# Attention with a token and channel mixer: q and k transposed by VectorE, scores as 32-row tiles, mixer input transposed by DMA

## The chip, the cores and the metric

The kernel runs on one core of one Trainium2 chip. The metric is the time of one execution on the device in microseconds (us); where a kernel ran several times, the median is quoted. Engine names in the profiles: PE is TensorE (PEld its weight loads), DVE is VectorE, ACT is ScalarE, POOL is GpSimd, and SP is the engine that issues most DMA transfers. In this kernel PE writes its results into PSUM, from where DVE or ACT copies them to tiles in SBUF. The clock of PE is given as the share of full speed that it was granted. Batches are counted from 0 here; the recorded expectations of the experiments count them from 1. One run of the kernel before took 840.59 us; it is left out of every ratio, but the medians 341.17 and 340.29 us on record still count it (without it they are 340.5 and 340.0). Runs marked slow (over 1.5% above the fastest of the same kernel) are left out of every ratio.

## The reference, cut to what matters

Eight batches of eight heads of causal attention with a decay that accumulates along the sequence (S = 576, D = 64), followed per batch by a mixer over tokens and one over channels.

```python
# shortened
scores = scale * np.matmul(q, k.transpose(0, 1, 3, 2))          # [8, 8, 576, 576]
cum = np.cumsum(np.maximum(s, 0.0), axis=-1)
bias = -(cum[:, :, :, None] - cum[:, :, None, :])
scores = np.where(causal, -1e9, scores + np.minimum(bias, 0.0))
attn = exp(scores - max); attn = attn / (sum + 1e-09)
x = np.matmul(attn, v)                                          # then heads side by side: [8, 576, 512]
# mixer
h  = np.maximum(x.T @ w_tok1, 0.0) @ w_tok2                     # w_tok1 576x256, w_tok2 256x576
u  = x + h.T
out = u + np.maximum(u @ w_ch1, 0.0) @ w_ch2                    # w_ch1 512x1536, w_ch2 1536x512
```

The kernel computes only two diagonals of 128x128 blocks of the attention (farther positions have decayed away, which a check at the end confirms; the squares of q and k serve that check).

## The kernel before

A small planner in the kernel takes every operation with its allowed engines and an estimate of its time, chooses the engine where there is a choice, and fixes the order of each engine before anything runs. The order cannot adapt when an operation takes longer than the estimate.

q and k are loaded for two heads, cast to bf16 (by GpSimd from batch 1 on), transposed by PE and copied out of PSUM by DVE or ACT:

```python
    def stage_qk(b, h):                      # two heads
        ...
            alts = {"POOL": (*c_pool(768, 0.0010), lambda cast=cast: cast(0))}
            if b == 0:
                alts["DVE"] = (*c_dve(768), lambda cast=cast: cast(1))
                alts["ACT"] = (*c_act(768), lambda cast=cast: cast(2))
    def pair(b, h):
        ...
                for r in range(R):           # R = 6
                    nc.tensor.transpose(out=o[:, r * PR : (r + 1) * PR],
                                        in_=nat.t[:, ti, r, :, :].rearrange("p e d -> p (e d)"), ...)
        ...                                  # kT and qT copied out of PSUM
                    nc.tensor.matmul(out=o[:, :, c0 : c0 + e - a], lhsT=kT.t[:, j0 : j0 + 128],
                                     rhs=qT.t[:, :, a:e], start=True, stop=True)
        ...                                  # Exp by ACT, then the causal mask by DVE:
                    nc.vector.tensor_tensor(
                        out=E.t[:, :, d0 : d0 + n], in0=E.t[:, :, d0 : d0 + n],
                        in1=keep[:, k0 : k0 + n].unsqueeze(1).to_broadcast([128, 2, n]), op=ALU.mult)
```

The score matmul uses all 128 rows of PE: the two heads lie above each other in kT, and qT holds zeros in the half of the other head. The causal mask reads two tensors in SBUF, E and keep. The input of the channel mixer (u transposed) is made by PE transposes and copies out of PSUM.

## Time and profile before

| | before |
|---|---|
| time, median | 341.17 us in the runs given (see above), 340.0 to 340.5 beside the experiments |
| span of the profiled run | 337.3 us |
| PE busy, PE idle | 315.2 us, 22.1 us |
| DVE / ACT / POOL busy | 207.7 / 221.6 / 100.1 us |
| first matmul of the channel mixer | 41.27 us |

Before the first matmul of the channel mixer PE also runs dummy matmuls, which are meant only to keep its clock up (no run here goes without them), so "PE busy" says little there. I therefore cut the time line at that matmul. In the view of the kernel before by stretches, the columns are the stretch, its length, then busy time and count of PE, PEld, DVE, ACT and POOL, the granted PE clock, the share of the DMA engines and GB/s:

```profile
41.27:110.00 68.73, 64.93 (x616) 43.33 (x620) 50.94 (x119) 50.97 (x94) 41.19 (x48) 1.00 0.91 207
110.00:230.00 120.00, 116.28 (x922) 65.53 (x935) 75.45 (x184) 84.36 (x147) 36.78 (x47) 1.00 0.51 132
230.00:337.30 107.30, 99.27 (x709) 56.51 (x716) 46.63 (x116) 59.16 (x110) 3.25 (x4) 1.00 0.26 79
```

Length minus PE busy is PE's idle time: 3.8, 3.7 and 8.0 us, together 15.6 us. PE is the bound after 41 us. The clock is full. One group of the same page: a third of the causal masks (those on one of three buffers), with count, busy time in us and mean in ns, then DVE's idle time before them:

```profile
L671 DVE TENSOR_TENSOR E_84<-E_84,keep 128x256 bf16<-128x256 bf16 (+1 forms) x55 | 18.4, 365 | 13.3 <-ACT E_84 L663 12.8
```

DVE waits for ACT's Exp before these masks. The masks are ready early enough that PE hardly waits for them: in the view of PE's waits the masks have two lines (total us, times, longest), 0.9 us together:

```profile
PE pav_115 L689 <- DVE E_84 L671: 0.6, 2, 0.3
...
PE pav_115 L689 <- DVE E_86 L671: 0.3, 1, 0.3
```

### The profile page before, as it was taken

The page shows a single profiled execution, that of the slowest core. Times are in us where ns is not written, and L with a number is a line of the kernel's source. Part 1 is how long each engine was busy: PE and PEld are TensorE (multiplying, and loading weights), DVE is VectorE, ACT ScalarE, POOL GpSimd, SP SyncE. Part 2 cuts the span into 40 slices and gives each one's busy share as a digit, 9 for nine tenths or more (in the row PEclk, how much of TensorE's full clock was granted, in tenths as well). Part 3 has the DMA queues.
Part 4 walks back from the last instruction along what each step waited for, and adds up shares of the span by engine and source line. Part 5 has one row for each costly group of instructions (what it writes and reads, how often), then busy time and mean ns, then how long its engine had stood idle before and what let it go on. Part 6 is the DMA issues. An engine that isn't in the chain of part 4 may idle for free.

```text
span 337.3 us, 6710 instructions
## 1 busy us (share of the span) xinstructions
PE 315.2 (93%) x2532; PEld 184.7 (55%) x2565; DVE 207.7 (62%) x510; ACT 221.6 (66%) x395; POOL 100.1 (30%) x137
## 2 busy tenths in 40 slices
PE   6978999988999999989999999989999999999992
PEld 2445585645765455555765445555765454446641
DVE  7698945899776746584577655584677545450021
ACT  4766975669788548785786747787799738325600
POOL 6355157768237001830147001830110000000000
PEclk9799999999999999999999999999999999999999
DMA  7999999999953349288024952253548110011031
GB/s 203 222 291 376 374 213 231 266 271 227 215 114 106 130 138 206 77 208 194 2 75 133 227 145 71 87 157 121 143 119 232 67 63 2 16 49 62 3 95 68
DMA packets 62584, 50.60 MB, mean 150 GB/s; under 512 B 39632, under 2 KB 55568, under 8 KB 62544
## 3 DMA queue, kind: packets, MB, share of 16 engines
q1 hardware_dynamic: 62544, 50.10, 56.7%
q8 instruction: 22, 0.36, 0.4%
q14 instruction: 18, 0.15, 0.2%
HBM read 40.65 MB, written 9.44 MB: 148 GB/s over the span
## 4 chain that ended last, share of the span: by engine, by line
PE 69%; DVE 18%; ACT 7%; issue 2%; DMA 1%; POOL 1%; SPq 0%; ACTq 0%
PE pmx_118 L877 9%; PE pmx_119 L877 8%; PE pmx_117 L859 8%; PE pmx_118 L859 8%; PE pmx_119 L859 8%; PE pmx_117 L877 7%; DVE ub_101 L819 3%; PE pmx_119 L791 2%; DVE E_86 L671 2%; PE psc_114 L657 2%; PE pav_115 L689 2%; PE psc_113 L657 2%; DVE E_84 L671 2%; PE pav_116 L689 2%; PE psc_112 L657 2%
## 5 line engine op out<-in xcount | busy, mean ns | idle before, releaser
L859 PEld LDWEIGHTS <-wc_70 128*128 128x128 bf16 x624 | 59.3, 98 | 30.5 <-issue 0.2
L877 PEld LDWEIGHTS <-gb_107 128*128 128x128 bf16 x240 | 22.9, 98 | 25.3
L575 POOL CAST qkn_76<-qkf_73 96x768 bf16<-96x768 f32 x22 | 19.1, 887 | 37.5 <-ACT gb_107 L866 20.1
L877 PEld LDWEIGHTS <-ga_106 128*128 128x128 bf16 x192 | 18.2, 98 | 21.2 <-issue 1.4
L575 POOL CAST qkn_77<-qkf_74 96x768 bf16<-96x768 f32 x19 | 15.7, 840 | 40.8 <-ACT ga_106 L866 19.7
L575 POOL CAST qkn_75<-qkf_72 96x768 bf16<-96x768 f32 x19 | 15.4, 828 | 39.1 <-ACT gb_107 L866 18.5
L671 DVE TENSOR_TENSOR E_84<-E_84,keep 128x256 bf16<-128x256 bf16 (+1 forms) x55 | 18.4, 365 | 13.3 <-ACT E_84 L663 12.8
L859 PE MATMUL pmx_118<-uTb_105,wc_70 128*128 128x320 bf16 x128 | 22.6, 299 | 0.1
L859 PE MATMUL pmx_117<-uTb_105,wc_70 128*128 128x320 bf16 x128 | 22.6, 299 | 0.0
L859 PE MATMUL pmx_119<-uTb_105,wc_70 128*128 128x320 bf16 x128 | 22.6, 299 | 0.0
L877 PE MATMUL pmx_119<-wc_71,gb_107 128*128 128x512 bf16 x92 | 22.3, 379 | 0.2
L548 POOL TENSOR_TENSOR vp_90<-vf_88,wT 128x512 bf16<-128x512 f32 (+1 forms) x20 | 21.0, 1069 | 2.5 <-DMA vf_88<-in_v_dram 2.2
L671 DVE TENSOR_TENSOR E_86<-E_86,keep 128x256 bf16<-128x256 bf16 (+1 forms) x50 | 17.1, 368 | 6.7 <-ACT E_86 L663 6.4
L671 DVE TENSOR_TENSOR E_85<-E_85,keep 128x256 bf16<-128x256 bf16 (+1 forms) x55 | 16.5, 329 | 6.3 <-ACT E_85 L663 6.1
L877 PE MATMUL pmx_118<-wc_71,gb_107 128*128 128x512 bf16 x80 | 19.2, 379 | 0.2
L866 ACT ACTIVATE gb_107<-pmx_119 128x320 bf16<-128x320 f32 x25 | 11.1, 444 | 11.4 <-PE pmx_119 L859 9.9
L859 PE MATMUL pmx_118<-uTa_104,wc_70 128*128 128x512 bf16 (+1 forms) x77 | 17.0, 335 | 0.2
L859 PE MATMUL pmx_119<-uTa_104,wc_70 128*128 128x512 bf16 (+1 forms) x79 | 17.1, 336 | 0.1
L548 POOL TENSOR_TENSOR vp_89<-vf_87,wT 128x512 bf16<-128x512 f32 (+1 forms) x15 | 15.3, 1040 | 5.8 <-PE pav_116 L689 4.7
L859 PE MATMUL pmx_117<-uTa_104,wc_70 128*128 128x512 bf16 (+1 forms) x78 | 16.8, 335 | 0.1
L877 PE MATMUL pmx_117<-wc_71,ga_106 128*128 128x512 bf16 x69 | 16.7, 379 | 0.2
L877 PE MATMUL pmx_118<-wc_71,ga_106 128*128 128x512 bf16 x69 | 16.5, 379 | 0.3 <-ACT uTb_105 L839 0.2
(297 smaller groups left out, 723.0 us busy)
## 6 DMA issues: line engine op xcount, KB each, us to landing
qkf_74<-in_k_dram SPq DMA_DIRECT2D x15, 288.0 KB, 3.4
qkf_74<-in_q_dram SPq DMA_DIRECT2D x15, 288.0 KB, 4.0
vf_87<-in_v_dram SPq DMA_DIRECT2D x16, 256.0 KB, 7.0
vf_88<-in_v_dram SPq DMA_DIRECT2D x16, 256.0 KB, 5.5
qkf_72<-in_k_dram SPq DMA_DIRECT2D x13, 288.0 KB, 4.0
qkf_72<-in_q_dram SPq DMA_DIRECT2D x13, 288.0 KB, 4.5
qkf_73<-in_k_dram SPq DMA_DIRECT2D x12, 288.0 KB, 4.7
qkf_73<-in_q_dram SPq DMA_DIRECT2D x12, 288.0 KB, 5.0
```

Of the source, the lines that this page charges most:

```text
L548: eng.tensor_tensor(out=vp.t[p0 : p0 + n, c, :, 0:D], in0=vf.t[p0 : p0 + n, c, :, :], in1=wT[p0 : p0 + n, cw, b * H : b * H + H].unsqueeze ...
L575: nc.gpsimd.tensor_copy(out=o, in_=a)
L657: nc.tensor.matmul(out=o[:, :, c0 : c0 + e - a], lhsT=kT.t[:, j0 : j0 + 128], rhs=qT.t[:, :, a:e], start=True, stop=True)
L671: nc.vector.tensor_tensor(out=E.t[:, :, d0 : d0 + n], in0=E.t[:, :, d0 : d0 + n], in1=keep[:, k0 : k0 + n].unsqueeze(1).to_broadcast([128, ...
L689: nc.tensor.matmul(out=o[:, ic, 0 : D + 1], lhsT=E.t[:, hh, d0 : d0 + 128], rhs=vp.t[:, jc, h + hh, 0 : D + 1], start=(jc == j_lo), stop=( ...
L791: nc.tensor.matmul(out=pm.t[:, ha * D : hb * D], lhsT=w1[:, NJ if odd and c == NJ - 1 else c, t * 128 : t * 128 + 128], rhs=x.t[:, c, ha * ...
L819: nc.vector.tensor_tensor(out=dst.t[lo:hi, di, :], in0=pm.t[lo:hi, :], in1=x.t[lo:hi, c, :], op=ALU.add)
L859: nc.tensor.matmul(out=pm.t[:, 0 : e - a], lhsT=wc1[:, m, cc * 128 : cc * 128 + 128], rhs=uT.t[:, m, a:e], start=(m == 0), stop=(m == NMC ...
L866: lambda cc=cc, pm=pm, a=a, e=e: nc.scalar.activation(out=g.t[:, cc, a:e], in_=pm.t[:, 0 : e - a], func=AF.Relu),
L877: nc.tensor.matmul(out=pm.t[:, :], lhsT=g.t[:, cc, c * 128 : c * 128 + 128], rhs=wc2[:, cc, :], start=(cc == 0), stop=(cc == NCC - 1))
```

## The change

The intent is to take work off PE. VectorE transposes q and k in 32x32 blocks, which leaves 32 of the 64 head elements on 32 partitions. Four heads therefore lie on the four row groups of PE, and each head's scores are two matmuls of 32 rows, accumulated in PSUM, that can run beside those of the other heads. The transposing, the rounding to bf16 and the reordering of the sequence are divided differently: the cast now also undoes the order of the loaded rows. From batch 2 on the mixer input is transposed by DMA.

```diff
-    R = 6
-    PR = S // R
+    UDMA = 2
+    HQ = 4
+    TP = 128 // HQ
+    R = S // TP
+    DQ = D // 32
 ...
     def stage_qk(b, h):
+        for i in range(2):
 ...
+            P.op(dve(R * D, lambda f=f, t1=t1: nc.vector.transpose(
+                out=t1.t[:, :, :, :].rearrange("p r q t -> p (r q t)"), in_=f.t[:, :])),
+                reads=[(f, 0)], writes=[(t1, 0)], holds=[T], prio=2 if b else -1)
+            for qq in range(DQ):
+                def cast(e, qq=qq, t1=t1, T=T):
+                    o = T.t[:, qq, 0:S].rearrange("p (t r) -> p t r", r=R)
+                    a = t1.t[:, :, qq, :].rearrange("p r t -> p t r")
+                    if e == 0:
+                        nc.gpsimd.tensor_copy(out=o, in_=a)
 ...
+                alts = {"POOL": (*c_pool(S, 0.0017), lambda cast=cast: cast(0))}
 ...
+                for (jc, a, z, c0) in cols:
+                    for qq in range(DQ):
+                        for e in range(HQ):
+                            p0 = e * TP
+                            nc.tensor.matmul(out=ps[e].t[:, c0 : c0 + z - a],
+                                             lhsT=kT.t[p0 : p0 + TP, qq, jc * 128 : jc * 128 + 128],
+                                             rhs=qT.t[p0 : p0 + TP, qq, a:z], start=(qq == 0), stop=(qq == DQ - 1),
+                                             tile_position=(p0, 0))
 ...
-                        in1=keep[:, k0 : k0 + n].unsqueeze(1).to_broadcast([128, 2, n]), op=ALU.mult)
+                        in1=keep[:, 0:n].unsqueeze(1).to_broadcast([128, HQ, n]), op=ALU.mult)
 ...
+            if b >= UDMA:
+                def xt(dst=dst, di=di, tc_=tc_):
+                    nc.sync.dma_start_transpose(out=uT.t[:, :, tc_ * 128 : tc_ * 128 + 128], in_=dst.t[:, di, :])
```

The diff also changes the loads (four heads at a time, fewer and larger packets), the squares (taken of the loaded fp32 values) and the number of buffers.

The read of the new cast steps 256 bytes from element to element: 18 values r, each a block of 64 fp32 apart. The write is contiguous.

## The prediction

> **What bounds the kernel now.** I first read the page's shares and slices, to see whether one engine is full.
>
> ```profile
> PE 315.2 (93%) x2532; PEld 184.7 (55%) x2565; DVE 207.7 (62%) x510; ACT 221.6 (66%) x395; POOL 100.1 (30%) x137
> ...
> PE   6978999988999999989999999989999999999992
> ...
> DMA  7999999999953349288024952253548110011031
> ```
>
> TensorE (PE) is busy 93% of the 337.3 us span, no other engine more than 66%. The DMA engines are full only in the first eleven slices (to about 93 us). So there are two stages. I checked this in the windows, whose columns are the stretch, its length, busy time and count of PE, PEld, DVE, ACT and POOL, the granted clock, the DMA share and GB/s:
>
> ```profile
> 0.00:20.00 20.00, 16.47 (x98) 7.79 (x100) 15.06 (x43) 12.42 (x21) 9.54 (x27) 0.91 1.03 224
> 20.00:40.00 20.00, 16.96 (x190) 11.00 (x191) 18.40 (x46) 13.47 (x24) 9.29 (x12) 1.00 1.03 351
> ...
> 160.00:180.00 20.00, 19.95 (x182) 13.50 (x182) 11.50 (x30) 15.09 (x31) 7.78 (x9) 1.00 0.20 60
> ```
>
> From 80 to 320 us PE is busy 234 of 240 us (sum of the twelve windows): there, each microsecond of PE work removed is a microsecond of time, as long as nothing else starts to wait. The first 41 us are different. The groups of line L964 are dummy matmuls on zeros that only keep the clock up; they sum to 19.1 us, all before 41.2 us. PE is not the limit there; the chain of waits between 5 and 32 us goes through VectorE (DVE) and ScalarE (ACT): casts, q/k evictions, Exp, mask, normalisation of batch 0. The first real mixer matmul (L859) starts at 41.27 us.
>
> What one piece of PE work really costs is not in the group means (they contain the pipeline's latency) but in the pieces of the chain of waits; the columns are start, length, engine, tile, line, count:
>
> ```profile
> 29.95 0.29 PE pav_115 L689 x9
> ...
> 32.38 0.26 PE psc_114 L619 x6
> 32.64 0.22 PE psc_112 L657
> 32.85 0.22 PE psc_113 L657
> ...
> 34.67 0.22 PE psc_114 L657
> 34.88 0.22 PE psc_112 L657 x2
> ...
> 37.82 0.22 PE pmx_119 L831 x4
> ```
>
> Six q/k transposes take 0.26 us, a 512-column score matmul 0.22, the last two (384 and 128 columns) 0.22 together, four transposes of the mixer input 0.22. The nine attention-value matmuls take 0.29, that is 32 ns for a weight load with its matmul, so weight loads can follow one another at least that fast.
>
> **What the skill says.** (1) "TensorE: Matmul & The Clock Gate", Part 3, gives 3.07x for four 32-row tiles at 512 columns, and says such matmuls overlap when each is in its own row group. No run here shows it yet. (2) "TensorEngine Tiling (Array Packing)", Key Properties: changing the tiling mode drains TensorE. The trace has no tiled matmul; its matmuls of 512 columns last 379 ns and follow each other every 216, so a drain is about 0.16 us. (3) "Vector Engine (DVE) Microarchitecture Reference", 3.8: the 32x32 transpose sustains one element per cycle and lane. The trace has none, but other one-rate operations: the 512-element products (L548) take 0.68 us, the 320-element ones (L703) 0.49, so 1.0 ns an element and 0.17 fixed. (4) "Advanced Engine Details and Errata", X-Bar Transpose (TRN2): transposing DMAs are as fast as plain ones. The trace has none.
>
> **The change, part by part.**
>
> *PE, scores.* Before, one pair of heads costs 2 x 0.26 + 4 x 0.22 = 1.40 us, four heads 2.80. After, q/k transposes leave PE altogether. Four heads are 40 matmuls of 32 rows: for each of two halves of the head's 64 elements 256+256+256+192+64 = 1024 columns on four row tiles. One tile alone would take 2 x 1024/2.4 GHz = 0.85 us; at 3.07 of the ideal 4, 1.11 us (an estimate from (1)). 40 loads at 32 ns give 1.28 as the other limit, from the trace. Two phases with a change of mode in and out are 4 drains of up to 0.16; I take half of them as exposed, 0.3. That is 1.4 to 1.6 us, say 1.5: saved 1.3 per four heads. Batch 0 lies before the matmuls that count, and three of the four pairs of batch 1 ran before 41 us beside dummies, so I count 12 of 16 groups: 12 x 1.3 = 15.6 us.
>
> *PE, mixer input.* Batches 2 to 7 have 3 x (4 + 5) = 27 tiles; each loses 0.22 us: 5.9 us, all in the full stage.
>
> *DVE and ACT.* Evictions of q/k: 36 on DVE at 0.75 and 60 on ACT at 0.64, 27 + 38 = 65 us, go. Evictions of the mixer input: 27 of 36 go (19 on ACT at 0.59, 17 on DVE at 0.41 in all), about 13.5 us. Squares: 32 x (1.48 + 0.19) = 53.5 becomes 32 x (1.48 x 1152/1536 + 0.19) = 41.6, minus 12. Masks: half as many, twice as wide; 160 at 0.33 are 52 us, and the 0.07 or so of fixed cost saved on 80 is 6 to 10. Added: 32 DVE transposes of 1152 elements at 0.17 + 1.15 = 1.32, plus 42 us. DVE and ACT together fall from 429 to about 375. Neither comes near the PE's some 290.
>
> *GpSimd.* 60 casts of 0.84 us (50 us) become some 56 strided ones of 576 elements. At the measured 1.08 ns an element they are 35 us; with the kernel's own allowance for strided reads 60. POOL goes to at most 115 of 310 us and stays off the path.
>
> *DMA.* The page has 62,584 packets, of which the 15,360 of q and k have 1536 bytes; afterwards there are 5,120 of 4608. By the kernel's own allowance two heads' k and q fall from 2.26 to 1.65 us, some 24 us of DMA time in all, of which six loads (about 3.5 us) lie ahead of the mixer's weights. Against that come 27 transposes of 128 KB.
>
> *Start.* Batch 0 loses two transposes and three evictions per pair from a chain that DVE and ACT bound, and gains four DVE transposes. Loads of 0.6 MB land near 5.5 and 7.2 us, first scores near 9.5 (before: 11.44), and four phases of four Exps (0.49 us apart in the timeline at 13 us) end near 20 to 21. I expect the normalised attention of batch 0 some 4 us earlier than 31.6, and the weights some 3.5 us earlier, so the first mixer matmul at about 37: 4 us.
>
> *New waits.* PE gets four score banks per phase and a phase fills all four, so phases follow at 2.5 us at best; with mixer work between, this is mostly hidden. A transposing DMA is issued in order on SyncE behind loads like these:
>
> ```profile
> 51.22 8.03 SPq L539 DMA_DIRECT2D vf_87<-in_v_dram  x5
> ```
>
> Five loads of v hold that queue for 8 us, while PE's order is fixed beforehand. I charge 4 us for late mixer input and score banks.
>
> Sum: 15.6 + 5.9 + 4 - 4 = 21.5 us. The median before is 341.17 (the 840.59 run is set aside), so 319.5.
>
> **The rivals.** (a) Row tiles do not overlap. Then four heads cost 4 x 0.85 + 0.3 = 3.7 us instead of 2.8: 12 x 0.9 = 11 us lost, with 5.9 + 4 - 4 gained: 346, within 2%. For it: no run here shows the overlap; against it: the skill's measured factor, and each tile has its own bank. (b) Mixer input arrives late: at 4 us of stall in each of six batches, 24 us instead of 4, leaving 339.5. For it: the 8 us above and the DMA share of 1 up to 93 us; against it: the DMA share falls to 0.2 to 0.7 after 100 us, and chan() of a batch is ranked behind two batches' attention, so other PE work stands in front. (c) Vector work becomes the bound: transposes of 1.32 us get between the masks and PE. Against it: 375 us on two engines over 320 us of span. If it does happen early (DVE is 18.40 of 20 us busy at 20 to 40 us), the start gives nothing: 323.5. (d) Everything overlaps and waits vanish too: 1.2 us per four heads, no new waits, 6 us at the start: 12 x 1.6 + 5.9 + 6 = 31, so 310.
>
> **Range and chances.** The sure part is PE work leaving a full PE. Centre 319; (d) with a little more gives 307, half of (b) with (c) gives 332. Faster by over 2% means below 334.3: it needs (a) or a full (b) to fail, 0.87. Within 2% 0.10, slower 0.03.
>
> **What would show it.** The 32-row matmuls of four heads spanning 1.4 to 1.6 us in two phases (3.7 would be rival a); PE busy time falling by 25 to 45 us with its idle time not up; the first L859-type matmul near 37 us; DVE transposes at 1.3 us; waits of the up-projection on the mixer-input DMA below 1 us each (several us would be rival b). The prediction fails if PE idle time after 80 us exceeds some 15 us, before about 6.

## The result and the profile after

The changed kernel took 323.82 us (median of five, 319.96 to 324.48), the kernel before beside it 340.29 us (340.0 without the run set aside). The ratio is 0.950, with a 95% interval of 0.944 to 0.955. Ratios here are the mean time of one kernel's fast runs over that of the other's in the same rounds, so not quite the ratio of the medians quoted. The profiled run happened to be the fastest of the five (span 318.2 us, clock 0.986); the others have spans of 320.4 to 322.6 us at a clock of 0.965 to 0.971.

The page of the changed kernel, first the busy times, then the slices of PE, its clock and DMA:

```profile
PE 288.5 (91%) x2550; PEld 162.1 (51%) x2550; DVE 220.6 (69%) x415; ACT 168.2 (53%) x319; POOL 121.7 (38%) x129
...
PE   7879999497888997998999999998899999999992
...
PEclk9999999798999999999999999999999999999998
DMA  7999999993797864024970597136960520050032
```

PE lost 26.7 us of work and ACT 53.4, while DVE and POOL gained 12.9 and 21.6. But in slices 8 to 19 (of 8 us each, so about 56 to 151 us) the row of PE has a 4, two 7s and four 8s, where the row before had three 8s and nothing below. PE's idle time in the whole span rose from 22.1 to 29.7 us. The same stretches as before, cut at the first mixer matmul, which is now at 33.57 us:

```profile
0.00:33.57 33.57, 27.94 (x284) 14.85 (x285) 30.46 (x70) 19.49 (x29) 16.11 (x29) 1.00 0.98 326
33.57:110.00 76.43, 66.05 (x726) 42.66 (x724) 66.91 (x121) 54.61 (x110) 53.89 (x51) 0.96 0.90 240
110.00:230.00 120.00, 112.65 (x970) 60.41 (x968) 88.37 (x148) 61.62 (x119) 51.59 (x49) 1.00 0.54 148
230.00:318.20 88.20, 81.81 (x575) 44.15 (x575) 34.84 (x79) 32.45 (x64) 0.08 (x1) 0.99 0.26 80
```

From the two tables the whole difference of the spans can be put together. The first mixer matmul is 7.7 us earlier. PE's busy time after it falls from 280.5 to 260.5 us, by 20.0. PE's idle time after it rises from 15.6 to 24.1 us, by 8.6 (10.4, 7.4 and 6.4 in the three stretches). -7.7 - 20.0 + 8.6 = -19.1 us, which is 337.3 to 318.2. This is bookkeeping, not yet a cause: an earlier start can be lost again in later waits.

What does PE wait for? The view of PE's waits in the changed kernel (total us, times, longest):

```profile
PE pmx L656 <- DVE E L638: 8.6, 9, 2.1
PE pmx L656 <- DVE x L670: 3.6, 2, 3.4
```

L656 is the attention-value matmul, L638 the causal mask. The masks are now the largest wait of PE; neither GpSimd nor a transposing DMA has a line in that view. And yet half as many masks, each twice as wide, should have been cheaper. The groups of the changed kernel that matter:

```profile
L582 POOL CAST kT<-qkt 128x576 bf16<-128x576 f32 x31 | 36.7, 1212 | 87.8 <-DVE qkt L574 76.0
...
L638 DVE TENSOR_TENSOR E<-E,keep 128x512 bf16<-128x512 bf16 (+1 forms) x80 | 55.0, 734 | 3.3 <-ACT E L631 3.2
```

The mask takes 734 ns in the mean. Its own view (shortest/median/longest in ns) shows that the mean is not typical:

```profile
L638 DVE TENSOR_TENSOR E<-E,keep x80: 273/426/1683, 14.2 to 266.1; 128x512 bf16<-128x512 bf16 x64, 128x256 bf16<-128x256 bf16 x16
```

Half of them take 426 ns or less, others up to four times that. The timeline around the deepest dip of PE shows when (start, length in us, engine, line, count; in brackets the idle time before it and its releaser):

```profile
54.86 2.30 POOL L582 CAST kT<-qkt 128x576 bf16<-128x576 f32 x2 [2.07 <-PE pmx L656]
56.63 3.26 DVE L638 TENSOR_TENSOR E<-E,keep 128x512 bf16<-128x512 bf16 x3
57.11 2.63 POOL L582 CAST qT<-qkt 128x576 bf16<-128x576 f32 x2
...
60.42 0.32 PE L656 MATMUL pmx<-vp,E 128*128 128x65 bf16 x3 [3.40 <-DVE x L670]
```

Three masks take 3.26 us, 1.09 each, while GpSimd casts run from 54.86 to 59.74. Behind them the normalisation (L670) is late, and PE stands still for 3.40 us. Just behind this gap the granted clock of PE was lower as well:

```profile
60.00:65.00 5.00, 4.58 (x59) 3.15 (x59) 3.93 (x13) 1.94 (x5) 5.00 (x7) 0.66 1.10 358
```

The Trainium skill, "SBUF — State Buffer", section "Who interferes with whom", names this: a VectorE instruction with two SBUF inputs contends with a GpSimd instruction that reads SBUF, because its second input comes through an interface that the two share. The mask is such an instruction and the cast such a reader; the timeline agrees, with 1.09 us against the median of 0.43.

The trace can settle this mask by mask. I sorted the 80 masks, from the start and length of each instruction in the trace, by whether a GpSimd cast or product was running when they started. The 35 beside none took 0.27 to 0.43 us. The other 45 took 1.00 us in the mean, and every one of them ended 0.15 to 0.31 us after that GpSimd instruction ended, however much of it was left. Of these 45, 31 started beside a cast of q or k, 10 beside a product for v and 4 beside other casts. So a mask that starts during such a GpSimd instruction waits for its end, and a longer one makes it wait longer. The kernel before shows the same on fewer masks: 30 of 160, with 0.71 us in the mean against 0.27.

The score phases did what was hoped. Timeline of PE in the changed kernel:

```profile
48.75 0.61 PE L622 MATMUL psc<-qT,kT 32*128 32x256 bf16 x16
49.30 2.76 PE L849 MATMUL pmx<-wc,ga 128*128 128x512 bf16 x12
51.99 0.62 PE L622 MATMUL psc<-qT,kT 32*128 32x256 bf16 x24
52.55 0.82 PE L849 MATMUL pmx<-wc,ga 128*128 128x512 bf16 x3
```

From the start of a phase to the start of the next matmul there are 0.55 and 0.56 us. Entering a phase costs some 0.1 us more: the 12 matmuls from 49.30 us, at 216 ns each, should be followed at 51.89, and the phase begins at 51.99. That is about 1.3 us for four heads, where the prediction's reading of the kernel before gave 2.80.

### The profile page after: what moved, and what is told of

Its sections match the earlier page's. It is cut to its first block, busy times and chain, and to the rows that moved or that the text cites. A ratio compares the mean times of both kernels' runs of the same rounds, so it can differ in the third digit from the quotient of the medians.

```text
span 318.2 us, 6568 instructions
## 1 busy us (share of the span) xinstructions
PE 288.5 (91%) x2550; PEld 162.1 (51%) x2550; DVE 220.6 (69%) x415; ACT 168.2 (53%) x319; POOL 121.7 (38%) x129
## 4 chain that ended last, share of the span: by engine, by line
PE 58%; DVE 27%; DMA 5%; issue 5%; SPq 1%; ACT 1%; DVEq 0%; ACTq 0%
PE pmx L831 23%; PE pmx L849 19%; DVE E L638 9%; DVE qkt L574 7%; PE pmx L758 5%; PE pmx L656 4%; DMA qkf<-in_q_dram 4%; PE psc L622 3%; PE pmx L779 2%; DVE ub L786 2%; DVE of L860 2%; DVE x L670 2%; DMA qkf<-in_k_dram 2%; DVE vp L543 1%; DVE ua L786 1%
## 5 line engine op out<-in xcount | busy, mean ns | idle before, releaser
L631 ACT ACTIVATE E<-psc 128x512 bf16<-128x512 f32 x128 | 66.1, 607 | 53.9 <-PE psc L622 53.9
L831 PEld LDWEIGHTS <-wc 128*128 128x128 bf16 x624 | 60.4, 98 | 35.9 <-issue 3.4
L831 PE MATMUL pmx<-uTb,wc 128*128 128x320 bf16 x384 | 55.0, 301 | 2.6 <-DVE gb L840 1.5
L638 DVE TENSOR_TENSOR E<-E,keep 128x512 bf16<-128x512 bf16 (+1 forms) x80 | 55.0, 734 | 3.3 <-ACT E L631 3.2
L849 PE MATMUL pmx<-wc,gb 128*128 128x512 bf16 x240 | 53.5, 379 | 0.0
L565 ACT ACTIVATE junk<-qkf 128x1152 bf16<-128x1152 f32 x32 | 37.6, 1174 | 14.1 <-DMA qkf<-in_k_dram 12.5
L849 PE MATMUL pmx<-wc,ga 128*128 128x512 bf16 x192 | 43.6, 379 | 0.0
L831 PE MATMUL pmx<-uTa,wc 128*128 128x512 bf16 (+1 forms) x240 | 43.5, 337 | 0.0
L574 DVE STREAM_TRANSPOSE qkt<-qkf 128x1152 f32<-128x1152 f32 x32 | 43.1, 1360 | 0.5 <-DMA qkf<-in_q_dram 0.2
L656 PE MATMUL pmx<-vp,E 128*128 128x65 bf16 x576 | 26.2, 196 | 16.9 <-DVE E L638 8.6
L543 POOL TENSOR_TENSOR vp<-vf,wT 128x512 bf16<-128x512 f32 (+1 forms) x35 | 37.1, 1090 | 8.7 <-PE pmx L656 8.7
L849 PEld LDWEIGHTS <-gb 128*128 128x128 bf16 x240 | 22.9, 98 | 26.7
L838 ACT ACTIVATE gb<-pmx 128x320 bf16<-128x320 f32 x58 | 24.9, 445 | 21.6 <-PE pmx L831 17.9
L656 PEld LDWEIGHTS <-E 128*128 128x128 bf16 x576 | 22.1, 99 | 24.3 <-issue 11.2
L670 DVE TENSOR_TENSOR x<-pmx,rc 128x320 bf16<-128x320 f32 x64 | 29.3, 484 | 0.8
L860 DVE TENSOR_TENSOR of<-pmx,ub 128x512 f32<-128x512 f32 x16 | 10.8, 687 | 15.0 <-PE pmx L849 12.9
## 6 DMA issues: line engine op xcount, KB each, us to landing
ga<-in_moe_w_ch_dram SPq DMA_DIRECT2D x2, 768.0 KB, 12.9
```

The lines of the kernel that those rows point to most:

```text
L543: eng.tensor_tensor(out=vp.t[0:n, c, :, 0:D], in0=vf.t[0:n, c, :, :], in1=wT[0:n, c, b * H : b * H + H].unsqueeze(2).to_broadcast([n, H, D ...
L565: P.op({"ACT": (1.1, 1.5, lambda: nc.scalar.activation(out=junk[:, :], in_=f.t[:, :], func=AF.Square, accum_out=sq[:, col : col + 1]))}, r ...
L574: P.op(dve(R * D, lambda f=f, t1=t1: nc.vector.transpose(out=t1.t[:, :, :, :].rearrange("p r q t -> p (r q t)"), in_=f.t[:, :])), reads=[( ...
L631: nc.scalar.activation(out=E.t[:, e, ph * 512 : ph * 512 + 512], in_=p.t[:, :], func=AF.Exp, scale=0.125)
L638: nc.vector.tensor_tensor(out=E.t[:, :, d0 : d0 + n], in0=E.t[:, :, d0 : d0 + n], in1=keep[:, 0:n].unsqueeze(1).to_broadcast([128, HQ, n]) ...
L656: nc.tensor.matmul(out=o[:, ic, 0 : D + 1], lhsT=E.t[:, hh, d0 : d0 + 128], rhs=vp.t[:, jc, h + hh, 0 : D + 1], start=(jc == j_lo), stop=( ...
```

## The experiments

The theory: the casts of q and k on GpSimd slow VectorE's masks beside them, and late masks leave PE idle. The main rival: something else that came with the change delays VectorE or PE, such as the 1.36 us transposes in front of the masks, late DMA transposes, or GpSimd itself being too slow for the scores. There were twelve runs, one of them the changed kernel again. The record marks every result as right, even that of casts_straight, which scrambles q and k. So this check does not notice a wrong order of q and k, and for the other runs that order rests on the code. The runs are ordered by question. Each has its own kernel-before runs of the same chip beside it (340.0 to 340.5 us in the median).

### Do the casts slow the masks?

**casts_act.** From batch 1 on ScalarE makes the casts, alone.

```diff
                 alts = {"POOL": (*c_pool(S, 0.0017), lambda cast=cast: cast(0))}
+                if b > 0:
+                    alts = {"ACT": (1.2, 1.4, lambda cast=cast: cast(2))}
```

> The changed kernel with the q/k casts of batches 2 to 8 on ScalarE in place of GpSimd. Theory (contention): the masks on VectorE take 0.73 us in the mean and 0.43 in the median because a GpSimd cast runs beside them; without casts on GpSimd their mean falls to about 0.5 (the v products still run there), VectorE busy falls by 15 us or more, and TensorE's idle time between 33 and 110 us falls from 10.4 to about 5; ratio to the kernel before near 0.935. Rival (VectorE is simply full with 32 transposes ahead of the masks in its order): the masks get shorter but TensorE's idle time stays above 9 us and the ratio stays at 0.95. Against both: ScalarE gains 56 casts of 1.2 us (67 us), so late Exps could take the gain back.

Measured: 312.61 us, ratio to the kernel before 0.919 (0.916 to 0.922). Its page, with the mask on line 640:

```profile
PE 285.8 (92%) x2520; PEld 161.6 (52%) x2549; DVE 219.1 (70%) x446; ACT 212.1 (68%) x344; POOL 54.4 (17%) x73
...
L640 DVE TENSOR_TENSOR E<-E,keep 128x512 bf16<-128x512 bf16 (+1 forms) x80 | 36.9, 510 | 6.9 <-ACT E L633 6.9
```

The mask's mean falls to 510 ns (80 take 36.9 us instead of 55.0). PE is idle 7.2 instead of 10.4 us between 33.57 and 110 us. ACT carries 44 us more and still does not become a bound. The gain is larger than forecast (0.935), but one forecast failed: DVE's busy time was to fall by 15 us or more and fell by 1.5. The masks did take 18.1 us less, but the new plan gave DVE 31 more instructions (446 against 415). It is 3 to 4% under the changed kernel and, within the noise, as fast as any run. One point against reading the start as decisive: its first mixer matmul comes at 38.94 us, 5.4 us later than in the changed kernel, and it ends 7 us earlier (profiled spans 311.2 and 318.2). The planner ordered everything anew here, though, so this run alone does not prove the mechanism.

**casts_half.** Only the casts of q go to ScalarE.

```diff
-                alts = {"POOL": (*c_pool(S, 0.0017), lambda cast=cast: cast(0))}
+                alts = {"POOL": (*c_pool(S, 0.0020), lambda cast=cast: cast(0))}
+                if b > 0 and i == 1:
+                    alts = {"ACT": (1.2, 1.4, lambda cast=cast: cast(2))}
```

> The changed kernel with the q casts (28 of 56) of batches 2 to 8 on ScalarE and the k casts left on GpSimd. Contention theory: mask mean near 0.6 us and about half of the gain of the run with all casts moved, unless ScalarE becomes late there, in which case this one is the fastest of the three: ratio 0.935 to 0.945. Rival (VectorE full): 0.95, unchanged.

Measured: 313.49 us, 0.924 (0.920 to 0.927); the mask's mean is 595 ns. Half the casts off GpSimd brings over 60% of the mask time back and most of the gain; the forecast of 0.935 to 0.945 was too cautious.

**after_again and casts_straight.** The control is the changed kernel itself. In casts_straight GpSimd reads and writes straight ahead, in the same number of elements, so that its casts become short; nothing is planned anew, every engine has the same instructions in the same order. What it computes is wrong.

```diff
-                        nc.gpsimd.tensor_copy(out=o, in_=a)
+                        nc.gpsimd.tensor_copy(
+                            out=T.t[:, qq, 0:S],
+                            in_=t1.t[:, :, :, :].rearrange("p r q t -> p (r q t)")[:, qq * S : qq * S + S])
```

> The changed kernel itself once more, as the control on this chip: a ratio of 0.950 to the kernel before, clock near 0.97, TensorE idle some 10 us between 33 and 110 us. Both theories expect the same.

> Wrong result on purpose: the GpSimd casts of q and k read and write straight through instead of in the strided order, with the same plan, the same order on every engine and the same number of instructions. A straight cast of 576 elements should take 0.6 to 0.7 us instead of 1.25. Theory (GpSimd casts beside the masks make them slow, not the order or the load of VectorE): with half the GpSimd cast time the mask mean falls from 0.73 to about 0.6 us and the ratio to 0.935 or 0.94 though nothing was re-planned. Rival (the run with the casts on ScalarE won because its plan put the instructions in another order): mask mean and ratio stay at 0.72 and 0.95. The scores are of scrambled q and k, which changes no instruction's size.

Measured: after_again 321.91 us, 0.948 (0.941 to 0.955), as in the first runs. casts_straight 312.57 us, 0.921 (0.914 to 0.929), better than the forecast of 0.935 or 0.94. The groups of casts_straight (the mask is on line 640 here):

```profile
L582 POOL CAST kT<-qkt 128x576 bf16<-128x576 f32 x31 | 20.2, 682 | 97.6 <-DVE qkt L574 88.0
...
L640 DVE TENSOR_TENSOR E<-E,keep 128x512 bf16<-128x512 bf16 (+1 forms) x80 | 43.3, 589 | 3.5 <-ACT E L633 3.3
```

Only GpSimd's casts were shortened, and DVE's masks became 11.7 us shorter. DVE's whole busy time fell by 11.9 us, so nothing else on DVE moved. Sorted as above, 35 masks instead of 45 start beside a GpSimd instruction, and they take 0.84 us instead of 1.00; those beside none take 0.40 us. The transposes, the DMAs and the order are the same, so the rivals that rest on them cannot explain it. The stretches of casts_straight:

```profile
33.57:110.00 76.43, 69.83 (x746) 44.40 (x743) 65.75 (x124) 55.30 (x111) 43.56 (x55) 0.96 0.90 245
110.00:230.00 120.00, 116.21 (x1032) 64.24 (x1030) 86.09 (x166) 66.66 (x128) 35.10 (x46) 1.00 0.57 163
```

PE is idle 6.6 and 3.8 us here, instead of 10.4 and 7.4: 7.4 of the 8.1 us by which the profiled spans differ (318.2 and 310.1). Both profiled runs have nearly the same mean clock (0.986 and 0.987). PE's waits for masks are halved, 4.3 us. What remains of the theory's rivals is that GpSimd itself was late; but the changed kernel's list of waits has no line of PE waiting for a cast on GpSimd, and DVE stood idle only 3.3 us before all its masks (3.5 in casts_straight), so it was not waiting for late scores either. This run settles it: the length of the casts beside the masks cost the changed kernel about 8 to 9 us (8.1 between the profiled runs, 9.3 between the medians). What the remaining overlap costs, with short casts and with the products for v, no run isolates.

**before_casts_act.** Is moving casts off GpSimd simply a good thing? The same on the kernel before, whose casts of 768 elements read runs of 64 neighbours.

```diff
             alts = {"POOL": (*c_pool(768, 0.0010), lambda cast=cast: cast(0))}
+            if b > 0:
+                alts = {"ACT": (0.85, 1.05, lambda cast=cast: cast(2))}
```

> The kernel before with its q/k casts of batches 2 to 8 on ScalarE too. Theory: the change itself made the contention matter, since there the masks take 0.33 us in the mean against 0.29 in the median and TensorE is full, so this gives nothing: ratio 0.99 to 1.01, or a little slower as ScalarE is the fuller engine there. Rival (moving casts off GpSimd is a gain of its own, unrelated to the change): ratio 0.97 to 0.98.

Measured: 338.29 us, 0.994 (0.988 to 1.000), as forecast; the mask's mean is 307 ns (354 in the kernel before, from its three groups). There PE waited only 0.9 us for masks, so shorter masks bring almost nothing. The slowing of masks was there already; that it costs time is new in the changed kernel.

**casts_order and casts_half_order.** The other way to write the same cast: read 32 fp32 side by side, write every 18th bf16. The idea was to make the cast shorter; casts_half_order does it with q's casts on ScalarE.

```diff
-                    o = T.t[:, qq, 0:S].rearrange("p (t r) -> p t r", r=R)
-                    a = t1.t[:, :, qq, :].rearrange("p r t -> p t r")
+                    o = T.t[:, qq, 0:S].rearrange("p (t r) -> p r t", r=R)
+                    a = t1.t[:, :, qq, :]
```

> The changed kernel, right result and same plan, with the two loops of each q/k cast exchanged: it now reads 32 neighbouring float32 and writes every 18th bf16, in place of reading every 64th float32 and writing 18 neighbours. If the far reads are what makes a GpSimd cast 1.25 us against 0.73 for a straight one, it takes 0.7 to 0.8 us now and the kernel behaves as the straight one did: mask mean near 0.6 us, ratio 0.92. If far writes cost as much as far reads, the casts stay at 1.2 us and the ratio at 0.948.

> Both at once: loops of the casts exchanged, and the q casts of batches 2 to 8 on ScalarE. If each removes GpSimd time beside the masks, the mask mean falls to 0.52 to 0.55 us, TensorE's idle time between 33 and 110 us falls below 7 us, and the ratio is 0.912 to 0.920, the best so far; if what is left is VectorE's own work, it stays at 0.92 as in the straight run.

Measured: 364.41 us, 1.070 (1.065 to 1.076; one slow run left out) and 352.44 us, 1.035 (1.029 to 1.040). Both are slower than the kernel before. The groups of casts_order:

```profile
L582 POOL CAST kT<-qkt 128x576 bf16<-128x576 f32 x31 | 80.8, 2805 | 73.0 <-DVE qkt L574 59.9
...
L638 DVE TENSOR_TENSOR E<-E,keep 128x512 bf16<-128x512 bf16 (+1 forms) x80 | 69.7, 918 | 3.2 <-ACT E L631 3.2
```

The hope fell: writing every 36 bytes makes the cast 2.3 times as long, and not on GpSimd alone, as ScalarE takes 2.77 us and VectorE 2.70 us for it. As a test of the theory the run is of use, because the dose went the other way. With GpSimd casts of 0.73, 1.25 and 2.84 us (mean of k and q) the mask's mean is 589, 734 and 918 ns. The time is not as clean here: in casts_order PE also waits 19.0 us for GpSimd's casts themselves, so its 1.070 is two effects. Nor does a mask wait for the end of such a cast here: masks that start beside one end up to 2.6 us before it, so the rule found above holds for the casts with far reads and not for these. Of casts_half_order's forecasts none came true; its mask mean is 767 ns.

### What is each part of the change worth?

**x_all_pe.** The changed kernel with PE transposes of the mixer input in all batches.

```diff
-    UDMA = 2
+    UDMA = 8
```

> The changed kernel with every transpose of the mixer input back on TensorE (none by DMA). Theory: the DMA transposes land in 2.5 us and nobody waits for them, so taking them away gives back their TensorE work, 27 x 0.22 = 5.9 us, a ratio near 0.967 against 0.950. Rival: TensorE idles some 10 us after 110 us anyway because VectorE is late, so the 5.9 us are hidden and the ratio stays within 0.945 to 0.955; or the extra evictions on VectorE and ScalarE make it cost more than 6 us.

Measured: 328.34 us, 0.965 (0.962 to 0.968). By the ratios (0.948 and 0.950 for the changed kernel) the DMA transposes are worth about 5 to 6 us on top of the scores part, as forecast.

**before_x_dma.** The kernel before, with the DMA transposes alone.

```diff
+            if b >= 2:
+                def xt(dst=dst, di=di, tc_=tc_):
+                    nc.sync.dma_start_transpose(out=uT.t[:, :, tc_ * 128 : tc_ * 128 + 128], in_=dst.t[:, di, :])
+                P.op({"SP": (1.3, 0, xt)}, reads=rk, writes=[(uT, c)], holds=[uT], prio=0, dma=0.7)
+                continue
```

> The kernel before with only the third part of the change: mixer input of batches 3 to 8 transposed by DMA. Theory: TensorE is full there from 80 us on, so the 27 x 0.22 us that leave it show one to one, 5.9 us or ratio 0.983, if nobody waits for the DMA; it was worth 1.5% in the changed kernel. Rival: in this kernel the loads hold the queue in other places, and the up-projections wait for late input: ratio 0.995 or more and waits of the up-projection on the DMA of a microsecond or more each.

Measured: 327.69 us, 0.963 (0.957 to 0.968): 12.5 us, twice what was expected, and a miss. Its page:

```profile
PE 309.0 (95%) x2457; PEld 178.0 (55%) x2457; DVE 208.1 (64%) x512; ACT 207.2 (64%) x366; POOL 102.2 (31%) x137
```

PE's busy time falls by 6.2 us, which is the predicted 5.9. The profiled spans differ by 11.5 us (337.3 and 325.8), so PE's idle time falls by the other 5.3, from 22.1 to 16.8. The parts are therefore not additive: the scores part alone brings 11.7 us (340.02 to 328.34, from x_all_pe), the DMA part alone 12.5, both together 16 to 18. Most of the saved idle time lies between 110 and 230 us, where PE is idle 0.5 us instead of 3.7. Which waits go there, and why, was not followed further and stays open.

### Do the row tiles overlap?

**tiles_in_turn.** The same score matmuls, but one head's tile after the other instead of turn by turn.

```diff
-                for (jc, a, z, c0) in cols:
-                    for qq in range(DQ):
-                        for e in range(HQ):
-                            p0 = e * TP
+                for e in range(HQ):
+                    for (jc, a, z, c0) in cols:
+                        for qq in range(DQ):
+                            p0 = e * TP
```

> The changed kernel with the same 40 score matmuls per four heads, but ordered head by head, so that neighbours use the same 32 rows of the array. Theory (the row tiles overlap, and that is what keeps the scores cheap): a phase that takes 0.55 us grows to near 2 x 4 x 512 columns / 2.4 GHz = 1.7 us; 12 groups of two phases on the full stage lose up to 2 x 1.15 x 12 = 28 us, less what the idle time absorbs: ratio 1.00 to 1.04. Rival (the matmuls hardly overlap; the gain is from the transposes that left TensorE): phases stay at 0.55 to 0.7 us and the ratio stays near 0.95.

Measured: 328.75 us, 0.968 (0.965 to 0.972), between the forecasts. The phase of 16 matmuls stays nearly as it was (mostly 0.58 us instead of 0.55). The phase of 24 more than doubles; timeline of PE in tiles_in_turn:

```profile
114.19 1.32 PE L622 MATMUL psc<-qT,kT 32*128 32x256 bf16 x24
115.45 0.82 PE L849 MATMUL pmx<-wc,gb 128*128 128x512 bf16 x3
```

It takes 1.26 us instead of 0.56. Without any overlap, 16 matmuls of 256 columns would need 1.7 us: matmuls of 512 columns follow each other every 216 ns in the kernel before (this is also the 2.4 GHz of the recorded texts), so 256 need about 0.108. The phase of 24 has as many columns in all. A phase of 0.56 us is thus overlap in fact, and it survives a head-by-head order with four matmuls of 256 columns per tile, but not with six of 256, 192 and 64. A queue of limited depth in front of each tile would do this; that is a conjecture, and no run here tells the number of matmuls from their lengths.

### Is there a better mix?

**casts_free.** The planner may choose GpSimd or ScalarE for each cast by its estimates.

```diff
-                alts = {"POOL": (*c_pool(S, 0.0017), lambda cast=cast: cast(0))}
+                alts = {"POOL": (*c_pool(S, 0.0020), lambda cast=cast: cast(0))}
+                if b > 0:
+                    alts["ACT"] = (1.2, 1.4, lambda cast=cast: cast(2))
```

> The changed kernel with each q/k cast of batches 2 to 8 planned on whichever of GpSimd and ScalarE is free first, with the measured cast times (1.25 and 1.2 us) in the plan. A candidate for a better version: both fixed splits came to 0.919 and 0.924, so 0.915 to 0.925; over 0.93 would say that the plan's idea of who is free does not help.

Measured: 315.51 us, 0.927 (0.921 to 0.933), just outside the 0.915 to 0.925 hoped for; the mask's mean is 621 ns. It is a little worse than casts_act (0.919). The planner has no term for what a GpSimd cast costs a mask.

**rows_apart.** From batch 3 on q and k are loaded in another order of rows, by four transfers per tensor, so that the casts go straight ahead with a right result; in batches 1 and 2 q's casts are on ScalarE.

```diff
+        def load_rows():
+            for e in range(HQ):
+                nc.sync.dma_start(out=f.t[e * TP : e * TP + TP, :].rearrange("t (r d) -> t r d", d=D),
+                                  in_=SRC[i][b, h + e, :, :].rearrange("(r t) d -> t r d", t=TP))
...
+                    if b >= ROWS:
+                        o, a = T.t[:, qq, 0:S].rearrange("p (r t) -> p r t", r=R), t1.t[:, :, qq, :]
```

> A candidate with a right result: from batch 4 on, q and k are loaded with every 32nd row to one partition, so that after VectorE's block transposes the columns already stand in token order and the GpSimd casts run straight; batches 2 and 3 keep the large packets and have their q casts on ScalarE. Expected: GpSimd casts near 0.7 us and a mask mean near 0.55 us from batch 4 on, ratio 0.915 to 0.925 as in the straight run. Rival: the 256-byte packets (3.2 us of DMA time a load by the packet time of v, in place of 1.65) and the longer issue on the load queue delay the mixer-input transposes behind them: waits of the up-projection on the DMA and a ratio of 0.94 or more.

Measured: 313.89 us, 0.921 (0.916 to 0.926). Its profile fell in a slow run, so I use only the fast times and, from the profile, mean durations: 758 ns for the q casts left on GpSimd, 891 for the k casts (11 of the 31 still have far reads), masks of 537 ns. By its code it keeps the right order, and it has the same ratio as casts_straight. casts_act is no slower and far simpler, so it is the version to keep.

## Why the prediction was right or wrong

The time was right: 319 predicted (from a base of 341.17 us, which still counts the run set aside), 323.82 measured, inside the range of 307 to 332 and on the likely side. The sum behind it was right in part only, and two of its errors cancelled by luck.

**Scores on PE: right.** Predicted 1.5 us for four heads, measured about 1.3. With the mixer input, 15.6 + 5.9 = 21.5 us of PE work were to go; 20.0 went after the first mixer matmul, though that cut lies at other places of the work in the two kernels, so the closeness proves little. Rival (a), no overlap, is refuted by the phases and by tiles_in_turn.

**Mixer input by DMA: right in this kernel.** 5.9 us predicted, about 5 to 6 measured by x_all_pe. That it brings 12.5 us alone was not foreseen. The view of the DMA issues of the changed kernel (count, size where known, median us from issue to landing) has a plain store of 128 KB beside the 128 KB transposes:

```profile
out_dram<-of SPq DMA_DIRECT2D x8, 128.0 KB, 2.4
...
uTb<-ub SPq DMA_TRANSPOSE x12, 2.5
```

They land equally soon, as the skill's statement in the prediction had it (how long each keeps the DMA engines busy was not compared). PE waits for none of them; rival (b) is refuted.

**Start: right direction, too small.** The last normalisation of batch 0 ends at 27.44 instead of 31.6 us, the 4 us predicted. The last cast of the up-projection's weights ends at 33.24 instead of 38.67 us, 5.4 instead of 3.5 earlier, and the first mixer matmul comes at 33.57 instead of the predicted 37. No run tests why. And casts_act, whose first mixer matmul came at 38.94 us, ended earlier all the same: these microseconds are not simply the kernel's.

**GpSimd: the step that failed.** The prediction put the casts at 35 to 60 us, POOL at "at most 115 of 310 us", and said that it "stays off the path". The casts took 1.21 to 1.29 us each, 72.0 us for 59, and POOL 121.7 us. PE indeed does not wait for GpSimd. But GpSimd lengthens the masks: the prediction's 42 to 46 us for them became 55.0, and PE waits for those. (Its saving of "6 to 10" us on 80 masks does not follow from its own 0.07 us each, which gives 5.6.) DVE and ACT together were put at about 375 us and came to 388.8; the masks are 9 to 13 us of that miss. The transposes were right (1.36 against 1.32 us).

**New waits: wrong place, and half the size.** 4 us were charged to late mixer input and full score banks. Neither shows in PE's waits. In their place the long casts, through late masks, cost some 8 to 9 us. The prediction's own signs showed it: PE's busy time fell by 26.7 us, within the 25 to 45 named, but its idle time was to be "not up" and rose by 7.6. After 80 us (to 300, 18 us before the end) about 11 us are idle, under the 15 named as failure; the prediction's "before about 6" leaves out the last 17 us as well. Up to the end it is 17.0, against 12.6 before. Rival (c), vector work as the bound early, is the nearest, though by GpSimd's reads rather than by the transposes. With the shorter casts of casts_straight the kernel takes 312.6 us, near rival (d). So the prediction was 7 us too cautious about the rest (319.5 against 312.6: the start came 3.7 us earlier than charged, and the 4 us of new waits did not come) and missed a cost of 8 to 9; the two errors largely cancelled.

**The clock, in part open.** Four of the five first runs ran at a clock of 0.965 to 0.971 and 2.3 to 4.5 us longer than the profiled one; casts_straight and casts_half ran at 0.977 to 0.992. Whether gaps of PE lower the clock stays open. Among the profiled runs the two do not follow each other closely: PE is idle 25.4 us at 0.972 in casts_act and 29.7 us at 0.986 in the changed kernel; only the extreme, casts_order, stands out with 53.5 us at 0.921.

## What to carry to other kernels

When work moves to an engine that is "off the path", ask not only whether that engine has time, but what it does to the engine next to it: a GpSimd copy of 1.25 us stretched VectorE instructions with two SBUF inputs from 0.43 to 1.09 us, and the wait in the profile names VectorE alone. A mask that starts beside such an instruction ends shortly after it, so what counts is the length of each GpSimd instruction beside the masks, not only their sum. A group whose mean is far above its median (734 and 426 ns here) is the sign to look at what runs beside its long members. The cleanest test shortens the suspect without touching the plan, even with a wrong result, as casts_straight did.

## What the Trainium skill lacked or had wrong

- "SBUF — State Buffer", "Who interferes with whom", names the contention of two-input VectorE instructions with GpSimd reads and calls it an exclusive lock, but has no measured case of such a pair. Here 45 masks of the changed kernel that start beside a GpSimd cast or product take 1.00 us in the mean and end 0.15 to 0.31 us after it, which agrees; the 35 others take at most 0.43 us. Shortening the casts alone was worth 8 to 9 us of 322. Beside the casts with far writes the lock does not last as long: masks ended up to 2.6 us before such a cast did.
- "GPSIMD Engine Reference", section 7, puts reads that step more than 8 bytes at 50% more, for custom kernels. The plain cast of 576 elements from fp32 to bf16 takes 0.73 us straight ahead and 1.25 us when it reads every 256 bytes, 70% more. The table has no row for writes: writing every 36 bytes takes 2.84 us, nearly four times, and ScalarE (2.77) and VectorE (2.70) pay it too.
- "TensorE: Matmul & The Clock Gate", Part 3, says that row tiles overlap; the phases here agree (16 matmuls of 256 columns in 0.55 us, 1.7 without overlap). It has no measurement of tiles issued one after the other: here four matmuls per tile in a row cost 0.03 us, while with six the phase takes 1.26 instead of 0.56 us.
